# Weight halves moved from GpSimd to VectorE and ScalarE, and gathers one expert further ahead, in a routed FFN kernel

## The chip, the cores and the metric

The kernel runs on one core of a Trainium2 chip. The metric is the device time of one execution in microseconds (us). The core's engines each work through a queue of their own in program order: TensorE (PE in the profile; its weight loads are PEld), VectorE (DVE), ScalarE (ACT), GpSimd (POOL) and SyncE (SP, here only a queue of DMAs). They wait for each other through semaphores. The tensors are in HBM, the tiles in SBUF, and TensorE writes into PSUM.

## The reference

Three blocks follow each other: attention in chunks of 64 tokens, a layer of eight experts, and a plain FFN.

```python
x = attention_in_chunks(q, k, v)          # [2304, 512], all heads side by side
logits = x @ w_gate                       # 8 experts
e = argmax(logits); gate = softmax(logits)[e]
# token i is kept if fewer than capacity = 576 earlier tokens chose its expert
h = relu(x[tokens of e] @ w1[e])          # w1[e]: [512, 1024]
out[tokens of e] = gate * (h @ w2[e])     # w2[e]: [1024, 512]
h = out @ w_in                            # [2304, 2048]
y = (h * sigmoid(h)) @ w_out              # [2304, 512]
```

With the inputs of the reference the eight experts get 512, 128, 466, 384, 174, 128, 320 and 192 tokens: 4, 1, 4, 3, 2, 1, 3 and 2 tiles of 128, twenty in all.

## The kernel before

Everything is computed in fp16 pairs. A matrix is scaled by a power of two and split into a high half (rounded to fp16) and a low half (the rest), and each product is made of three matmuls: high by high, high by low, low by high. The power of two of a weight matrix comes from the sum of its squares. `w_prep(e, m, hi_eng, lo_eng)` returns the five steps of this for matrix m (0 is w1, 1 is w2) of expert e, each matrix in four chunks of [128, 1024]:

- `sq(c)`: ScalarE squares a chunk and sums along the row (L162);
- `red`: one TensorE matmul with ones adds the partitions (L122);
- `sc`: VectorE makes the scale from it (L168, L100 to L102), called the scale below;
- `hi(c)`: the high half of a chunk by `hi_eng` (L175 on ScalarE, L177 on another engine);
- `lo(c)`: the low half by VectorE (L180), from the chunk, the scale and the high half.

For expert 0 the high halves are made by ScalarE, for all others by GpSimd.

An expert's tokens are worked off in tiles of 128. `gather(e, j)` (L830) is an indirect DMA on GpSimd's queue that fetches the rows of tile j into a buffer `xg`. `x_tr(e, j)` transposes it by eight TensorE transposes (L842) into the one PSUM buffer `xtp`, which ScalarE copies to SBUF as `mxT` (L843). `t_f1` (L837) makes the rows' factor on VectorE. `tile_a(e, j)` is the upper tile, the first matrix: two halves of 48 matmuls (L858), each followed by ScalarE's Relu (`hh`, L863) and VectorE's rest (`hl`, L864). `tile_b(e, j)` is the lower tile, the second matrix: 24 matmuls of 512 columns (L884), then the eviction: a square for the norm (L893) and a scaled copy (L895) by ScalarE, the scale in between and the low half (L897) by VectorE, and a scatter on GpSimd's queue (L900).

The order is written out by hand (`manual_schedule`): what the text of the kernel issues first is first in each engine's queue. An expert runs as tile_a(0), tile_a(1), tile_b(0), tile_a(2), tile_b(1), and so on, under branches on its number of tokens (`more`); an expert with one tile runs tile_a(0), tile_b(0) and then the list `arms[0]`. Work for the next experts is put in between. `slots` are the places of the first tile: 0 ahead of tile_a, 1 after its first half, 2 after its end, 4 ahead of the last quarter of tile_b(e, 0), 5 behind it. `arms[j]` are the places of tile j: 0 to 2 within tile_a(j) likewise, 3 behind it, 5 behind tile_b(j−1). `nxt0(3)`, `nxt0(0)`, `nxt0(2)` and `nxt0(1)` come after tile_a's first half, after its end, at the middle and at the last quarter of tile_b(e, 0).

While expert e runs, the halves of expert e+1 are made (`hi1`, `lo1` of w1 and `hi2`, `lo2` of w2), and the squares of expert e+2 (`sq1`, `sq2`). `cb` and `cn` are pieces of the preparation of the FFN's first matrix: three VectorE operations (L805, L808, L813, a conversion) and ScalarE's norm (L819).

Of the kernel before, what the change touches and what calls it, by code (L numbers as in the profile page):

```python
# [8 lines left out]
F32 = mybir.dt.float32  # L9
# [13 lines left out]
def attention_moe_ffn_kernel(  # L23
# [617 lines left out]
    act_copy = nc.scalar.copy  # L641
    prep = {(1, m): w_prep(1, m, nc.gpsimd, nc.vector) for m in range(2)}
    p10 = prep[1, 0]
# [125 lines left out]
    mps = m_pool("mps", 1, space=PSUM)  # L769
    xg_s = [m_p.tile([P, XW], F32, name=f"xg{i}") for i in range(4)]  # L770
    xT_s = [m_p.tile([P, 2 * KD, P], F16, name=f"mxT{i}") for i in range(4)]
    f1_s = [m_p.tile([P, 1], F32, name=f"yf1{i}") for i in range(5)]
    hh_s = [m_p.tile([P, 4, P], F16, name=f"hh{i}") for i in range(4)]
# [23 lines left out]
    def f_conv(k):  # L797
        m, c = divmod(k, KFF)
        t = fs_s[k % 2]
        d = (win, wot)[m][:, c + 1, :]  # L800
        di = d.bitcast(I32)
        lo_w, hi_w = t[:, :, 0], t[:, :, 1]

        def b1():
            nc.vector.tensor_scalar(di, hi_w, 3, 0x3FFFFFFF, ALU.logical_shift_left, ALU.bitwise_and)  # L805

        def b2():
            nc.vector.scalar_tensor_tensor(  # L808
                out=di, in0=hi_w, scalar=-1073741824, in1=di, op0=ALU.bitwise_and, op1=ALU.bitwise_or
            )  # L810

        def b3():
            nc.vector.scalar_tensor_tensor(  # L813
                out=di, in0=lo_w, scalar=29, in1=di, op0=ALU.logical_shift_right, op1=ALU.bitwise_or
            )
            f_load(k + 2)

        def norm():
            nc.scalar.activation(  # L819
                out=(win, wot)[m][:, 0, :], in_=d, func=ACTF.Square, accum_out=fn2[:, m, c:c + 1]  # L820
            )

        return b1, b2, b3, norm
# [4 lines left out]
    def gather(e, j, idx):  # L828
        t = xg_s[2 * (e % 2) + j % 2]
        nc.gpsimd.indirect_dma_start(  # L830
            out=t, out_offset=None, in_=x_d[:, :], in_offset=bass.IndirectOffsetOnAxis(ap=idx, axis=0)
        )

    def t_f1(e, j):
        xg = xg_s[2 * (e % 2) + j % 2]
        f1 = f1_s[e % 2 if j == 0 else 2 + j % 3]
        nc.vector.tensor_scalar(f1, xg[:, DM:DM + 1], w_fac[e, 0], w_fac[e, 1], ALU.mult, ALU.mult)  # L837

    def x_tr(e, j):
        xh = xg_s[2 * (e % 2) + j % 2].bitcast(F16)  # L840
        for c in range(2 * KD):
# [29 lines left out]
    def tile_b(e, j, tok_i, c_i, keep, nxt, bg):  # L871
        f1, b = f1_s[e % 2 if j == 0 else 2 + j % 3], w_sp[e, 1]
        yp = yp_s[j % 2]
# [57 lines left out]

    g_next(0, 0)
    t_next(0, 0)
    g_next(0, 1)
    g_next(1, 0)
    w_load(1, 1)
    w_load(2, 0)
# [3 lines left out]
    for c in range(4):  # L941
        p10[3](c)
    n_e = [nc.values_load(cnt_i[0:1, e:e + 1], min_val=0, max_val=NT) for e in range(E)]

    for i in range(28):
        nc.tensor.matmul(out=ps_s[2][:, i % 4, :], lhsT=ones16, rhs=ident16)

    def more(e, j, arms, nxt0, bg0):
        def nxt(k):
            if k == 0 and j + 1 < NJ:  # L950
                x_tr(e, j + 1)
                t_f1(e, j + 1)
            if k == 0 and j + 2 < NJ:
                g_next(e, j + 2)
# [51 lines left out]
    for e in range(E):  # L1006
# [6 lines left out]
        if e + 2 < E:  # L1013
            for m in range(2):
                prep[e + 2, m] = w_prep(e + 2, m, nc.gpsimd, nc.vector)

# [13 lines left out]
        if not last:  # L1030
            sq1, sq2 = part(e + 2, 0, 0), part(e + 2, 1, 0)
            lo1, lo2 = los(0), los(1)
            hi1, hi2 = part(e + 1, 0, 3), part(e + 1, 1, 3)
            g2, gn = lambda: g_next(e, 2), lambda: g_next(e + 1, 1)
            if e == 0:
                sq = part(1, 1, 0)
                slots[1] = [lo1[0], *sq[0:2]]
                slots[2] = [*sq[2:4], gn, lambda: w_load(2, 1), *lo1[1:4]]
                slots[4] = [*scale(1, 1), *hi2]
                arms[0] = [*lo2, *sq1, *scale(2, 0), *sq2, *cb]  # L1040
                arms[1] = [[], [], [*cb[0:1]], [], [], [*lo2, *sq1]]
                arms[2] = [[], [], [*cb[1:]], [], [], [*scale(2, 0), *sq2]]
            else:
                slots[0] = [lambda: g_next(e + 1, 0), *hi1]
                slots[1] = [lo1[0], *sq1[0:2]]
                slots[2] = [*scale(e + 1, 1), g2, gn, *hi2, *sq1[2:4], *cn_prev, *lo1[1:4]]
                slots[5] = scale(e + 2, 0)
                arms[0] = [*lo2, *sq2, *cb]
                arms[1] = [lo2[0:1], [lo2[1], *sq2[0:2]], [*lo2[2:4], *sq2[2:4], *cb[0:1]], [], [], []]
                arms[2] = [[], [], [*cb[1:]], [], [], []]  # L1050
# [5 lines left out]
        def nxt0(k):  # L1056
            if k < 0:
                return
            if k == 3:
                x_tr(e, 1)  # L1060
            elif k == 2:
                if not last:
                    x_tr(e + 1, 0)
            elif k == 0:
                t_f1(e, 1)
                if last:
                    g_next(e, 2)
            elif not last:
                t_f1(e + 1, 0)
            else:  # L1070
                with tc.If(n_e[e] <= SPLIT0):
# [221 lines left out]
```

## Time and profile before

| | us |
|---|---|
| median of 3 runs | 858.53 (858.44 to 860.61) |
| profiled execution | 857.81 |
| its span, first to last instruction | 856.0 |
| mean granted clock of TensorE | 0.940 |
| busy: TensorE, VectorE, ScalarE, GpSimd | 731.6, 459.3, 358.9, 370.7 |

The attention and the routing end at about 146 us, the experts run to 443 us, and the FFN takes the rest. The granted clock is a share of 2.4 GHz: 1.00 is 2.4 GHz and 0.50 is 1.2 GHz. A row of the timeline gives the start, the duration, the engine, the line and the operation, the tiles (written from read), the shapes and the count; in brackets stands how long the engine was idle before it, and what ended that.

### The profile page before, as it was taken

To read this page: it belongs to the slowest core of one execution; us is meant where nothing else is said; L and a number is where in the kernel's file an instruction comes from. 1 tells how busy PE (TensorE), PEld (TensorE's weight loads), DVE (VectorE), ACT (ScalarE), POOL (GpSimd) and SP (SyncE) were. 2 spreads that over 40 slices of the span, in tenths; PEclk is the share of its full clock that TensorE was granted. 3 is DMA by queue.
4 is the path that set the end of the run, shared out by engine and by line. 5 is a ranking of instruction groups with operands and counts; after the bars stand their busy time and mean duration, and the time that the engine had idled before them with its cause. 6 is when DMAs were issued, how large, how long until landed. Compare 5 with 4: busy or idle time off the path is not lost. (4 is left out here: it accounts for less than half of the span.)

```text
span 856.0 us, 15037 instructions
## 1 busy us (share of the span) xinstructions
PE 731.6 (85%) x5750; PEld 444.2 (52%) x5750; DVE 459.3 (54%) x920; ACT 358.9 (42%) x643; POOL 370.7 (43%) x355
## 2 busy tenths in 40 slices
PE   5787753898789887869978777999999999999995
PEld 4676642875656655565733333444444444565442
DVE  4465586664992848699339999544332222212000
ACT  4586638475742726542424455332232223223010
POOL 3564541444961818486157644444223222312111
PEclk9899885899989998998999999899999999999998
DMA  7989891991892546433524246020001000000001
GB/s 168 235 227 202 193 234 39 342 348 46 275 292 63 185 166 198 145 99 87 129 59 98 67 131 148 1 49 1 1 26 50 0 1 38 13 1 38 13 34 41
DMA packets 103763, 95.94 MB, mean 112 GB/s; under 512 B 55904, under 2 KB 82528, under 8 KB 103648
## 3 DMA queue, kind: packets, MB, share of 16 engines
q1 hardware_dynamic: 97216, 76.07, 32.7%
q0 software_dynamic: 5760, 18.39, 6.6%
q8 instruction: 64, 1.05, 0.5%
q14 instruction: 51, 0.42, 0.2%
q10 hardware_dynamic: 672, 0.02, 0.0%
HBM read 73.45 MB, written 14.71 MB: 103 GB/s over the span
## 5 line engine op out<-in xcount | busy, mean ns | idle before, releaser
L1181 PE MATMUL ops<-wot,gh 128*128 128x512 f16 x576 | 171.3, 379 | 0.0
L1153 PE MATMUL fh<-yT,win 128*128 128x512 f16 (+1 forms) x768 | 157.7, 356 | 7.5 <-DVE g L1164 7.5
L1168 POOL TENSOR_TENSOR gl<-g,gh 128x512 f16<-128x512 f32 (+1 forms) x80 | 91.5, 1146 | 164.4 <-ACT gh L1166 164.4
L1153 PEld LDWEIGHTS <-win 128*128 128x128 f16 x960 | 94.5, 99 | 117.8 <-issue 26.2
L858 PE MATMUL mh<-mxT,wsp 128*128 128x128 f16 x1920 | 113.1, 220 | 8.8 <-ACT yr L893 4.1
L858 PEld LDWEIGHTS <-wsp 128*128 128x128 f16 x1920 | 110.5, 99 | 11.7 <-issue 10.4
L884 PE MATMUL myp<-wsp,hh 128*128 128x512 f16 x320 | 104.5, 411 | 12.6 <-issue 6.0
L1160 ACT ACTIVATE th<-th,fi 128x512 f32<-128x512 f32 (+1 forms) x80 | 54.3, 679 | 134.9 <-DVE th L1159 134.0
L1159 DVE TENSOR_TENSOR th<-fh,rb 128x512 f32<-128x512 f32 (+1 forms) x64 | 39.8, 622 | 131.1 <-PE fh L1153 131.1
L1181 PE MATMUL ops<-wot,gl 128*128 128x512 f16 x288 | 109.2, 379 | 0.0
L1181 PEld LDWEIGHTS <-gh 128*128 128x128 f16 x576 | 56.4, 98 | 64.1
L1166 ACT CAST gh<-g 128x512 f16<-128x512 f32 (+1 forms) x80 | 45.9, 574 | 76.5 <-DVE g L1164 57.6
L1164 DVE TENSOR_TENSOR g<-fh,th 128x512 f32<-128x512 f32 (+1 forms) x80 | 50.7, 634 | 39.9 <-ACT th L1160 32.1
L884 PE MATMUL myp<-wsp,hl 128*128 128x512 f16 x160 | 64.9, 406 | 0.0
L900 POOL DMA_INDIRECT y_d<-yr,tabs x20 | 21.4, 1070 | 94.3 <-DVE yr L892 30.9
L180 DVE SCALAR_TENSOR_TENSOR wsp<-st,s,wsp 128x1024 f16<-128x1024 f32 x40 | 60.4, 1551 | 2.1 <-POOL wsp L177 2.1
L177 POOL TENSOR_SCALAR wsp<-st,s 128x1024 f16<-128x1024 f32 x32 | 56.6, 1784 | 8.2 <-issue 7.5
L884 PEld LDWEIGHTS <-hh 128*128 128x128 f16 x320 | 32.4, 105 | 51.0 <-issue 17.4
L830 POOL DMA_INDIRECT xg<-x_d,tabs x34 | 44.3, 1304 | 26.9 <-issue 6.2
L1153 PE MATMUL fh<-st,win 128*128 128x512 f16 x192 | 43.4, 379 | 9.4 <-DVE g L1164 9.0
L180 DVE SCALAR_TENSOR_TENSOR wsp<-wot,s,wsp 128x1024 f16<-128x1024 f32 x24 | 44.9, 1916 | 8.2 <-POOL wsp L177 8.2
L1181 PEld LDWEIGHTS <-gl 128*128 128x128 f16 x288 | 28.2, 98 | 33.9
(201 smaller groups left out, 1013.3 us busy)
## 6 DMA issues: line engine op xcount, KB each, us to landing
st<-in_moe_w_dram SPq DMA_DIRECT2D x40, 512.0 KB, 4.6
wot<-in_moe_w_dram SPq DMA_DIRECT2D x24, 512.0 KB, 5.6
fs<-in_moe_w_in_dram SPq DMA_DIRECT2D x16, 512.0 KB, 7.4
fs<-in_moe_w_out_dram SPq DMA_DIRECT2D x16, 512.0 KB, 5.2
vbd<-in_v_dram SPq DMA_DIRECT2D x72, 64.0 KB, 3.9
x_d<-xr SPq DMA_DIRECT2D x9, 512.0 KB, 6.9
ku<-in_k_dram SPq DMA_DIRECT2D x6, 512.0 KB, 4.5
qu<-in_q_dram SPq DMA_DIRECT2D x6, 512.0 KB, 8.4
```

The lines of the kernel that those rows point to most:

```text
L177: hi_eng.tensor_scalar(sp[c][:, 0, :], st[c], s, 1.0, ALU.mult, ALU.mult)
L180: lo_eng.scalar_tensor_tensor(out=sp[c][:, 1, :], in0=st[c], scalar=s, in1=sp[c][:, 0, :], op0=ALU.mult, op1=ALU.subtract)
L830: nc.gpsimd.indirect_dma_start(out=t, out_offset=None, in_=x_d[:, :], in_offset=bass.IndirectOffsetOnAxis(ap=idx, axis=0))
L858: nc.tensor.matmul(out=ps[:, f4, :], lhsT=a[c][:, part, f0:f0 + P], rhs=xt[:, rc, :], start=(n == 0), stop=(n == 3 * KD - 1),)
L884: nc.tensor.matmul(out=yp, lhsT=lh[:, f % 4, :], rhs=b[f // 2][:, part, (f % 2) * DM:(f % 2 + 1) * DM], start=(n == 0), stop=(n == 3 * KF1 ...
L1153: nc.tensor.matmul(out=hp[:, 0:n], lhsT=wv[:, part, c, :], rhs=yT_t[b](rc, n), start=(i == 0), stop=(i == 3 * KD - 1),)
L1159: nc.vector.tensor_tensor(out=th[:, 0:n], in0=hp[:, 0:n], in1=rb_t[b][:, 0:n], op=ALU.mult)
L1160: nc.scalar.activation(out=th[:, 0:n], in_=th[:, 0:n], func=ACTF.Sigmoid, scale=fi[:, 0:1])
L1164: nc.vector.tensor_tensor(out=g[:, 0:n], in0=hp[:, 0:n], in1=th[:, 0:n], op=ALU.mult)
L1166: nc.scalar.copy(out=gh[:, 0:n], in_=g[:, 0:n])
L1168: nc.gpsimd.tensor_tensor(out=gl[:, 0:n], in0=g[:, 0:n], in1=gh[:, 0:n], op=ALU.subtract)
L1181: nc.tensor.matmul(out=o_t[b][t], lhsT=lh[:, t * P:(t + 1) * P], rhs=wv[:, part, :], start=(f == 0 and i == 0), stop=(f == KFF - 1 and i = ...
```

## The change

- High halves: of w1 by VectorE and of w2 by ScalarE, for experts 2 to 7; for expert 1, w1 by GpSimd as before and w2 by ScalarE.
- Gathers: six buffers `xg`, two for each of three experts. The first two tiles of expert e+2 and the third of e+1 are asked for at `nxt0(1)` of expert e, the fourth of e in its own slot 2.
- The transposes of expert e+1's second tile move into the last quarter of expert e's tile_b(e, 0), right behind those of the first tile at its middle. For that, `xT_s[0]` and `xT_s[2]` lie in parts of `win` and `wot`, and the norm of the conversion writes to `junk` instead.
- At the start both first gathers, the loads of the token counts into registers and the warm-up matmuls (48 instead of 28) come ahead of the first transposes.
- The order in the slots is written anew.

```diff
-    prep = {(1, m): w_prep(1, m, nc.gpsimd, nc.vector) for m in range(2)}
+    prep = {(1, m): w_prep(1, m, (nc.gpsimd, nc.scalar)[m], nc.vector) for m in range(2)}
...
-    xg_s = [m_p.tile([P, XW], F32, name=f"xg{i}") for i in range(4)]
+    xg_s = [m_p.tile([P, XW], F32, name=f"xg{i}") for i in range(6)]
+    xT_s = [None if i % 2 == 0 else m_p.tile([P, 2 * KD, P], F16, name=f"mxT{i}") for i in range(4)]
+    xT_s[0], xT_s[2] = (r.bitcast(F16).rearrange("p (c t) -> p c t", c=2 * KD) for r in (win[:, 0, :], wot[:, KFF, :]))
...
-                out=(win, wot)[m][:, 0, :], in_=d, func=ACTF.Square, accum_out=fn2[:, m, c:c + 1]
+                out=junk[:, 0:512] if m == 0 else wot[:, 0, :], in_=d, func=ACTF.Square, accum_out=fn2[:, m, c:c + 1]
...
     g_next(0, 0)
+    g_next(0, 1)
+    n_e = [nc.values_load(cnt_i[0:1, e:e + 1], min_val=0, max_val=NT) for e in range(E)]
+
+    for i in range(48):
+        nc.tensor.matmul(out=ps_s[2][:, i % 4, :], lhsT=ones16, rhs=ident16)
     t_next(0, 0)
-    g_next(0, 1)
     g_next(1, 0)
+    g_next(1, 1)
...
-            if k == 0 and j + 2 < NJ:
+            if k == 0 and j + 2 < NJ and (j > 1 or e + 1 == E):
                 g_next(e, j + 2)
...
-                prep[e + 2, m] = w_prep(e + 2, m, nc.gpsimd, nc.vector)
+                prep[e + 2, m] = w_prep(e + 2, m, (nc.vector, nc.scalar)[m], nc.vector)
...
             if e == 0:
                 sq = part(1, 1, 0)
-                slots[1] = [lo1[0], *sq[0:2]]
-                slots[2] = [*sq[2:4], gn, lambda: w_load(2, 1), *lo1[1:4]]
-                slots[4] = [*scale(1, 1), *hi2]
+                slots[1] = [lo1[0], sq[0]]
+                slots[2] = [g3, sq[1], lambda: w_load(2, 1), *lo1[1:4]]
+                slots[4] = [*sq[2:4], *scale(1, 1), *hi2]
                 arms[0] = [*lo2, *sq1, *scale(2, 0), *sq2, *cb]
-                arms[1] = [[], [], [*cb[0:1]], [], [], [*lo2, *sq1]]
-                arms[2] = [[], [], [*cb[1:]], [], [], [*scale(2, 0), *sq2]]
+                arms[1] = [[], [], [], [], [], [*lo2, *sq1, *cb[0:1]]]
+                arms[2] = [[], [], [*scale(2, 0)], [*sq2], [], [*cb[1:]]]
             else:
-                slots[0] = [lambda: g_next(e + 1, 0), *hi1]
-                slots[1] = [lo1[0], *sq1[0:2]]
-                slots[2] = [*scale(e + 1, 1), g2, gn, *hi2, *sq1[2:4], *cn_prev, *lo1[1:4]]
+                slots[0] = [hi1[0], hi1[1], lo1[0]]
+                slots[1] = [hi1[2], lo1[1], *sq1[0:1]]
+                slots[2] = [*scale(e + 1, 1), g3, hi1[3], *hi2[0:2], *lo1[2:4], *cn_prev]
+                slots[4] = [*sq1[1:4]]
                 slots[5] = scale(e + 2, 0)
-                arms[0] = [*lo2, *sq2, *cb]
-                arms[1] = [lo2[0:1], [lo2[1], *sq2[0:2]], [*lo2[2:4], *sq2[2:4], *cb[0:1]], [], [], []]
+                arms[0] = [*hi2[2:4], *lo2, *sq2, *cb]
+                arms[1] = [[], [], [], [*hi2[2:4], *lo2[0:2]], [], [*lo2[2:4], *sq2, *cb[0:1]]]
                 arms[2] = [[], [], [*cb[1:]], [], [], []]
...
             if k == 3:
-                x_tr(e, 1)
+                if e == 0:
+                    x_tr(e, 1)
...
             elif not last:
+                x_tr(e + 1, 1)
                 t_f1(e + 1, 0)
+                t_f1(e + 1, 1)
+                for g in ((e + 1, 2), (e + 2, 0), (e + 2, 1)):
+                    if g[0] < E:
+                        g_next(*g)
```

`g2`, `gn` and `g3` are gathers: the third tile of e, the second of e+1, and the fourth of e.

## Rows read from the trace of the kernel before

**Rows 1.** Groups of TensorE, 146 to 443 us: busy, mean ns, idle before, releasers.
```profile
L858 PE MATMUL mh<-mxT,wsp 128*128 128x128 f16 x1920 | 113.1, 220 | 8.8 <-ACT yr L893 4.1 <-DVE ye L100 3.1 <-ACT mxT L843 1.2
L884 PE MATMUL myp<-wsp,hh 128*128 128x512 f16 x320 | 104.5, 411 | 12.6 <-issue 6.0 <-ACT junk L162 3.4 <-POOL wsp L177 3.2
L842 PE MATMUL fh<-ident,xg 128*128 128x128 f16 x224 | 19.2, 235 | 23.0 <-DMA xg<-x_d,tabs 23.0
```

**Rows 2.** Timeline of TensorE at the start of the experts.
```profile
150.44 1.03 PE L842 MATMUL fh<-ident,xg 128*128 128x128 f16 x8 [4.47 <-DMA xg<-x_d,tabs]
...
153.88 3.08 PE L946 MATMUL mh<-ident,ones 128*128 128x128 f16 x28 [2.08 <-issue]
156.80 2.84 PE L858 MATMUL mh<-mxT,wsp 128*128 128x128 f16 x48
```

**Rows 3.** Timeline of TensorE, expert 2: transposes of the third tile.
```profile
238.32 1.04 PE L842 MATMUL fh<-ident,xg 128*128 128x128 f16 x8 [5.85 <-DMA xg<-x_d,tabs]
```

**Rows 4.** Stretches: us, busy of PE, PEld, DVE, ACT, POOL, PEclk, DMA share, GB/s.
```profile
239.10:243.20 4.10, 4.10 (x15) 1.59 (x13) 4.10 (x3) 3.21 (x5) 4.10 (x3) 0.63 0.91 311
243.60:246.25 2.65, 2.65 (x17) 1.33 (x15) 2.65 (x5) 1.01 (x1) 2.55 (x2) 1.00 0.90 267
...
sum 35.56, PE 35.52 PEld 16.70 DVE 34.92 ACT 19.11 POOL 33.58; mean PE 3.95 PEld 1.86 DVE 3.88 ACT 2.12 POOL 3.73
```

**Rows 5.** Timeline of VectorE, experts 0 and 1.
```profile
163.99 0.69 DVE L864 SCALAR_TENSOR_TENSOR hl<-mh,hh 128x512 f16<-128x512 f32 x1 [1.73 <-ACT hh L863]
...
164.77 3.67 DVE L180 SCALAR_TENSOR_TENSOR wsp<-st,s,wsp 128x1024 f16<-128x1024 f32 x3
...
169.74 0.42 DVE L805 TENSOR_SCALAR win<-fs 128x512 int32<-128x512 int32 x1
...
170.92 0.69 DVE L813 SCALAR_TENSOR_TENSOR win<-fs,win 128x512 int32<-128x512 int32 x1
...
208.29 4.31 DVE L180 SCALAR_TENSOR_TENSOR wsp<-wot,s,wsp 128x1024 f16<-128x1024 f32 x1 [1.61 <-POOL wsp L177]
```

**Rows 6.** Timeline of TensorE and GpSimd, expert 0, lower tile 0 to upper tile 3.
```profile
172.74 0.28 PE L122 MATMUL fh<-n,ones 128*128 128x4 f32 x2
...
173.76 6.54 POOL L177 TENSOR_SCALAR wsp<-st,s 128x1024 f16<-128x1024 f32 x4 [6.89 <-issue]
...
174.18 5.52 PE L858 MATMUL mh<-mxT,wsp 128*128 128x128 f16 x96
...
179.54 0.61 PE L842 MATMUL fh<-ident,xg 128*128 128x128 f16 x8
179.98 0.59 PE L884 MATMUL myp<-wsp,hh 128*128 128x512 f16 x2
...
185.16 0.28 PE L122 MATMUL fh<-n,ones 128*128 128x4 f32 x2
```

**Rows 7.** Two lines' instructions: duration in ns, least, median, most; first and last start.
```profile
L425 DVE TENSOR_SCALAR xr<-x,xs x4: 488/488/679, 119.6 to 130.8; 128x512 f16<-128x512 f32 x4
...
L175 ACT ACTIVATE wsp<-st,s x8: 1132/1137/1150, 91.1 to 149.3; 128x1024 f16<-128x1024 f32 x8
```

**Rows 8.** Timeline of ScalarE, expert 0, from the last copy in lower tile 0.
```profile
171.65 1.01 ACT L843 COPY mxT<-fh 128x1024 f16<-128x1024 f16 x1 [1.98 <-PE fh L842]
...
174.38 0.60 ACT L893 ACTIVATE yr<-myp 128x512 f16<-128x512 f32 x1 [1.72 <-PE myp L884]
...
176.12 1.05 ACT L162 ACTIVATE junk<-wot 128x1024 bf16<-128x1024 f32 x1
...
180.71 1.06 ACT L863 ACTIVATE hh<-mh 128x512 f16<-128x512 f32 x2
```

**Rows 9.** Line L122, the sum over squares: waits of its engine (us, times).
```profile
  ACT junk L162: 3.1, 3
```

**Rows 10.** Groups of VectorE, 146 to 443 us, columns as in rows 1.
```profile
L180 DVE SCALAR_TENSOR_TENSOR wsp<-st,s,wsp 128x1024 f16<-128x1024 f32 x36 | 54.9, 1570 | 2.1 <-POOL wsp L177 2.1
L180 DVE SCALAR_TENSOR_TENSOR wsp<-wot,s,wsp 128x1024 f16<-128x1024 f32 x24 | 44.9, 1916 | 8.2 <-POOL wsp L177 8.2
```

## What I expected before the run

> **What bounds the kernel now.** I began with the groups of TensorE in the expert stage (146 to 443 us), because the change touches nothing behind it. Between two experts, or within one, TensorE stands still in four ways. Transposes of gathered tokens wait for the gather, 23.0 us in all [rows 1]. 4.5 us of it is the very first gather [rows 2]; the other 18.5 us are five waits in experts 2, 3, 4 and 6, the longest 5.85 us [rows 1, 3]. Three waits are for the halves of weights: 3.2 in expert 1, 3.4 in expert 5 and 3.1 at the start of expert 6 [rows 1]. One is for a ScalarE copy, 1.2 [rows 1]. What is called issue comes back unchanged.
>
> Each of the seven longer waits leaves TensorE at the half level (1.2 of 2.4 GHz) for a while: twelve wide matmuls (or half an upper tile) take 4.10 us at a granted clock of 0.63, and 2.65 at 1.00 [rows 4]. Nine such stretches are 35.52 us together, two of them undisturbed (2.61 and 2.65); the seven slow ones are so 30.3 us where 18.6 would do, 11.7 lost [rows 4]: 7.2 behind gathers, 4.5 behind weights. Four transposes at the half level cost 0.4 each, 1.7.
>
> Next I looked at why weights and gathers are late. GpSimd makes the high halves, and VectorE's low half (two SBUF inputs) then takes 4.31 us, where three in a row alone take 3.67 [rows 5]. The gathers stand behind these halves in GpSimd's queue.
>
> **What the change takes away.** With gathers asked for an expert ahead, each has at least one lower and one upper tile (5.2 and 5.4 us [rows 6]) before its use, and GpSimd has nothing else from expert 1 on but scatters. I count all five waits as gone: 18.5 + 7.2 + 1.7 = 27.4. The three weight waits, with their clock: 3.2 + 3.4 + 3.1 + 4.5 = 14.2. The copy: 1.2. At the start the register loads (2.08) and the warm-up come ahead of the first transposes, so inside the 4.5 us wait. Before, 28 of them took 3.08 at the half level, and the level rose at 156.80 [rows 2]. Now they can start about 148.7; I let 48 end at 153.6 with the level risen, transposes at 154.1, a copy of 1.0, and the first tile at 155.2 for 156.80: 1.6 (0 if the level rises as late as before, 2.5 at best). Together 44.4 us.
>
> At this place a page speaks for the change: the Trainium skill, GPSIMD Engine Reference, Specifications, has GpSimd's SBUF interfaces shared with VectorE, in conflict with two-input instructions. The 4.31 us agree. The price is in the sum from the rows already.
>
> **What the change adds.** Four high halves of the first matrix per expert on VectorE. No such instruction of 1024 elements is in the trace; the same operation on 512 takes 0.488 [rows 7]. Bounds: 0.68 (twice it less a fixed part) and 1.2 (the pace of a low half); I take 0.7, nearest to the like operation. The Trainium skill, VectorE: DVE Perf Modes, section Mode 2×_2P, says that one-source fp32 between SBUF operands passes two results a cycle; 0.488 agrees. Four of the second matrix on ScalarE: exactly this instruction is there, 1.137, one begun every 1.04, so 4.3 for four [rows 7]. No total is too large; the order is what hurts. ScalarE works in order, and its queue holds the squares (1.15 each [rows 8]), the copies of transposes (1.0), the evictions and now the halves. TensorE waits for it in two places: the sum over the squares (L122, three waits already [rows 9]), and the next transposes, which need the one PSUM buffer `xtp` that the copy empties. The diff moves three squares to the last quarter of tile_b, behind them the second tile's copy, and the second matrix's halves behind VectorE's scale.
>
> Terms: half an upper tile 2.7, upper tile 5.36, transposes 0.45, lower tile 5.2, a quarter of it 1.3; matmul of sums to the next engine's start 1.02 [rows 6]. On VectorE: low half 1.2, hl 0.69, a conversion 0.42 + 0.73 + 0.69, with gaps 1.87 [rows 5]. Eviction on ScalarE 1.8 from its start to the next operation [rows 8].
>
> *Expert 0.* T is the last quarter of tile_b(0,0), 172.74 in the old trace; the copy before it ends then [rows 6, 8]. Squares 2 and 3 follow, so the sums wait to T+2.3: 2.3 lost. Scale, then four halves: T+3.4 to T+7.7; copy of expert 1's second tile to T+8.7; eviction to T+10.6; the four squares of expert 2 to T+15.4. TensorE goes on at T+2.7: transposes, the quarter, tile_a(0,2), transposes: T+10.1. There now stands the sum over those squares (formerly only after the next lower tile, at 185.16): 5.3 lost, and 1.3 for the clock. 8.9.
>
> *Experts 1 and 5 (one tile).* Count from the first matmul. VectorE ends the old eviction at 1.9, then two halves, a low half, hl, a half, a low half, hl: 7.8, scale 8.5. ScalarE's two halves wait for it and end at 10.7, two norms (0.7 each, squares of 512 columns like the eviction's 0.60 [rows 8]) 12.1, copy of the next expert's first tile 13.1. TensorE would transpose the second tile at 9.9: 3.2 lost. The three squares end at 16.7, TensorE's quarter, at half level, at 14.9: 1.8 lost. 5.0. In expert 5 VectorE is 3 us later (expert 4's last conversion and eviction): 2.5 before the lower tile, 3.85 and 1.75: 8.1.
>
> *Experts 2 and 6 (after one tile).* ScalarE comes with an eviction, two halves and four squares in hand: these end at 9.1, TensorE's upper tile at 5.4 (3.8 lost, 1.3 clock). VectorE has four low halves, two conversions, three high halves, two low, two hl before the scale: 3.0 + 4.8 + 3.7 + 2.1 + 2.4 + 1.4 + 0.7 = 18.1. ScalarE's halves, norms, two Relus and copy follow to 23.9; TensorE wants `xtp` at 19.4: 4.5. The next copy ends at 27.0, wanted at 25.7: 1.4. In expert 2 the squares end at 30.6, wanted at 28.9: 1.75. 12.8 and 11.0.
>
> *Experts 3 and 4.* Scale at 8.5 as in expert 1; TensorE has a second upper tile to do meanwhile, so 0.3 for `xtp`, then 1.45, then 1.75 for the squares: 3.5 each.
>
> *Expert 7* has no next expert: nothing. Transposes that move from one expert to the one before cost the same in both.
>
> **Sum.** New: 8.9 + 5.0 + 12.8 + 3.5 + 3.5 + 8.1 + 11.0 = 52.8. Removed: 44.4. Net +8.4 on the profiled execution's 857.8 gives 866.2; the median of the runs is 0.7 above that execution, so 867 us. The FFN behind it starts later by the same amount, with the same conversions left; its own waits stay. `xT` in `win` and `wot` is a change of place only; the norm's output in `junk` is written by the engine that writes it already.
>
> **Rivals.** (1) Faster: VectorE, freed from GpSimd, is so far ahead that the scale is there when ScalarE comes to the halves. VectorE's 60 low halves lose 28 us of contention (99.8 busy [rows 10] against 60 x 1.2) and take on 24 x 0.7 = 17. Then 3.2 in expert 1, 6.3 in expert 5, 6.0 in 2 and 6, and 1.7 in 3 and 4 vanish: 52.8 − 25 = 28, net −16, 842. For it: that surplus. Against it: the surplus lies in places where VectorE waits, in order, for ScalarE's evictions. The same goes for the page on GpSimd above: followed alone, it leads here. (2) Slower still: high halves at 1.2 on VectorE. It decides where the scale comes last: three halves ahead of it, 1.5 later, in six experts: +9, 876. Against it: 0.488. (3) About even: the half level does not follow the new waits (−3.9), and scale and squares come a little sooner than by my sums (−0.4 to −0.8 in each of six experts): 858 to 861. (4) The change does not do what it says: gathers that stand behind VectorE's factors (L837) are late again. They would have to be over 10 us late; I give it nothing apart.
>
> **Chances.** Forecast 0.60 (its own range 861 to 873), faster rival 0.18, slower still 0.12, about even 0.10. What a measurement here can tell from no change is 0.3%, 2.6 us. So faster 0.18, same 0.10, slower 0.72. For 8 in 10 the range takes the forecast, the even case and the slower one and part of the way to the faster: 853 to 877.
>
> **What would show it.** In the new trace: no wait of L842 for a gather after the first; low halves near 1.28 throughout; L177 on VectorE at about 0.75; the sum L122 after tile_a(0,2) waiting 5 us for ScalarE's squares; L842 waiting for the copy L843, in experts 2 and 6 by 4 to 5 us; ScalarE idle before L175 until VectorE's L102. Wrong if ScalarE does not wait before L175, or if L122 finds its squares done: then the removed 44 us stand alone and the kernel is much faster.

## The result and the profile after

The changed kernel takes 869.0 us (median, 866.5 to 870.3), 858.5 before: 1.0115 of it, with a 95% interval of 1.0082 to 1.0147. That is slower, as forecast, and 2 us from the 867.0. But that the number came out was luck, for it came of two wrong halves: what was taken away gave much less than the sum's 44 us, and what was added cost much less than its 53.

The profiled execution took 868.9 us (before: 857.8), its span 867.1. Line numbers have moved by one or two: what was L842, L843, L858, L884, L893 and L895 is now L843, L844, L859, L885, L894 and L896; the branches on an expert's number of tokens, L961 before, are L963. The first matmul of the experts comes at 156.27 us for 156.80, and the FFN begins at 454.4 for 443.4. The whole loss of 11 us so lies in the expert stage. The columns of the next rows are the stretch, its length, then busy time (and instructions) of TensorE, its weight loads, VectorE, ScalarE and GpSimd, the granted clock, DMA share and GB/s; the kernel before first.

```profile
156.80:443.42 286.62, 245.31 (x2656) 176.86 (x2653) 192.61 (x347) 141.63 (x261) 159.32 (x117) 0.93 0.54 175
```

The same of the changed kernel:

```profile
156.27:454.39 298.12, 246.00 (x2652) 176.53 (x2652) 177.09 (x371) 170.60 (x289) 68.46 (x67) 0.95 0.54 171
```

GpSimd lost 91 us of work, ScalarE got 29, VectorE lost 16 net. TensorE's busy time is the same within 0.7 us, so the loss is in its waits. Its groups in the changed kernel, 146 to 455 us (busy, mean ns, idle before, releasers), answer to [rows 1]; L859 has three rows now, since `xT` lies in three tiles.

```profile
L885 PE MATMUL myp<-wsp,hh 128*128 128x512 f16 x320 | 102.7, 405 | 16.9 <-issue 6.7 <-DVE wsp L180 3.3 <-DVE t L168 2.9
...
L859 PE MATMUL mh<-win,wsp 128*128 128x128 f16 x672 | 39.1, 219 | 2.1 <-ACT win L844 1.0 <-ACT yr L894 0.8 <-issue 0.3
L859 PE MATMUL mh<-mxT,wsp 128*128 128x128 f16 x672 | 38.5, 219 | 1.6 <-ACT yr L894 1.6
L859 PE MATMUL mh<-wot,wsp 128*128 128x128 f16 x576 | 36.4, 230 | 0.0
L843 PE MATMUL fh<-ident,xg 128*128 128x128 f16 x224 | 17.9, 225 | 10.2 <-ACT win L844 9.2 <-ACT mxT L844 1.0
L122 PE MATMUL fh<-n,ones 128*128 128x4 f32 x28 | 5.2, 254 | 20.2 <-ACT junk L162 20.2
L938 PE MATMUL mh<-ident,ones 128*128 128x128 f16 x48 | 4.4, 278 | 3.9 <-DVE tabs L709 3.9
```

The 23.0 us for gathers are gone. In their place the sums L122 wait 20.2 us for ScalarE's squares (0.1 before in this stretch; the 3.1 of [rows 9] lie outside it) and the transposes 10.2 us for ScalarE's copy (before, none did; the 1.2 there are upper tiles that waited for it). The waits ahead of the lower tile's matmuls, 6.6 of whose 12.6 us I had counted out, have not gone down but up, to 16.9.

The timeline of TensorE at the start, answering to [rows 2]: the warm-up stands ahead of the transposes, but it begins at 150.27 and not at 148.7. The row names VectorE's tables (L709) as the releaser. What ended last is something else: the eight loads of token counts into registers on TensorE's own queue (L935), which run from 146.90 to 150.25. The warm-up begins 4.1 us after the routing's last matmul (L691) here, and 1.9 in experiment 9, which has no such loads.

```profile
150.27 4.40 PE L938 MATMUL mh<-ident,ones 128*128 128x128 f16 x48 [3.91 <-DVE tabs L709]
154.51 0.61 PE L843 MATMUL fh<-ident,xg 128*128 128x128 f16 x8
```

The loads on TensorE's queue (ns least, median, most; first and last start):

```profile
L935 PEldq TENSOR_LOAD <-cnt_i x8: 300/306/499, 146.9 to 149.9; - x8
```

In expert 0, answering to [rows 6], the two sums wait where the prediction put them, 2.03 and 4.03 us:

```profile
174.41 0.39 PE L122 MATMUL fh<-n,ones 128*128 128x4 f32 x2 [2.03 <-ACT junk L162]
...
186.94 0.39 PE L122 MATMUL fh<-n,ones 128*128 128x4 f32 x2 [4.03 <-ACT junk L162]
```

In expert 2, the same view: a wait for squares, an upper tile that runs 7.15 us for 5.52, and a wait for the copy out of `xtp`. The transposes of the third tile, which waited 5.85 us for a gather in [rows 3], come at 244.68 without a wait; those that wait for the copy, at 251.94, are of expert 3's first tile.

```profile
237.45 0.38 PE L122 MATMUL fh<-n,ones 128*128 128x4 f32 x2 [3.54 <-ACT junk L162]
237.70 7.15 PE L859 MATMUL mh<-wot,wsp 128*128 128x128 f16 x96
244.68 0.61 PE L843 MATMUL fh<-ident,xg 128*128 128x128 f16 x8
...
251.94 0.61 PE L843 MATMUL fh<-ident,xg 128*128 128x128 f16 x8 [4.06 <-ACT win L844]
```

The cause of the second wait stands in ScalarE's timeline of that stretch. ScalarE sits idle for 7.06 us until VectorE has the second matrix's scale (L101), then makes two halves (L175), two norms and two Relus, and only then the copy that TensorE has wanted since 247.9.

```profile
246.46 2.19 ACT L175 ACTIVATE wsp<-st,s 128x1024 f16<-128x1024 f32 x2 [7.06 <-DVE s L101]
248.56 0.61 ACT L820 ACTIVATE junk<-win 128x512 bf16<-128x512 f32 x1
...
249.92 1.06 ACT L864 ACTIVATE hh<-mh 128x512 f16<-128x512 f32 x2
250.88 1.01 ACT L844 COPY win<-fh 128x1024 f16<-128x1024 f16 x1
```

### The profile page after: what moved, and what is told of

The parts are those of the page before. It is cut to its first block, busy times and chain, and to the rows that moved or that the text cites. A ratio compares the mean times of both kernels' runs of the same rounds, so it can differ in the third digit from the quotient of the medians.

```text
span 867.1 us, 14949 instructions
## 1 busy us (share of the span) xinstructions
PE 735.1 (85%) x5770; PEld 446.6 (52%) x5770; DVE 443.8 (51%) x944; ACT 388.2 (45%) x671; POOL 280.8 (32%) x305
## 5 line engine op out<-in xcount | busy, mean ns | idle before, releaser
L885 PE MATMUL myp<-wsp,hh 128*128 128x512 f16 x320 | 102.7, 405 | 16.9 <-issue 6.7
L859 PEld LDWEIGHTS <-wsp 128*128 128x128 f16 x1920 | 112.2, 100 | 6.7 <-issue 4.8
L831 POOL DMA_INDIRECT xg<-x_d,tabs x36 | 38.2, 1060 | 112.4 <-issue 80.1
L885 PE MATMUL myp<-wsp,hl 128*128 128x512 f16 x160 | 64.5, 403 | 0.7 <-issue 0.7
L885 PEld LDWEIGHTS <-hh 128*128 128x128 f16 x320 | 31.8, 103 | 52.9 <-issue 21.8
L180 DVE SCALAR_TENSOR_TENSOR wsp<-st,s,wsp 128x1024 f16<-128x1024 f32 x40 | 50.6, 1300 | 0.0
L162 ACT ACTIVATE junk<-st 128x1024 bf16<-128x1024 f32 x40 | 42.2, 1056 | 3.7 <-DMA st<-in_moe_w_dram 3.0
L100 DVE TENSOR_SCALAR ye<-yn 128x1 int32<-128x1 int32 x20 | 3.1, 154 | 79.2 <-ACT yr L894 79.2
L859 PE MATMUL mh<-win,wsp 128*128 128x128 f16 x672 | 39.1, 219 | 2.1 <-ACT win L844 1.0
```

Source lines behind the costliest of these rows:

```text
L162: nc.scalar.activation(out=junk, in_=st[c], func=ACTF.Square, accum_out=n2[:, c:c + 1])
L180: lo_eng.scalar_tensor_tensor(out=sp[c][:, 1, :], in0=st[c], scalar=s, in1=sp[c][:, 0, :], op0=ALU.mult, op1=ALU.subtract)
L831: nc.gpsimd.indirect_dma_start(out=t, out_offset=None, in_=x_d[:, :], in_offset=bass.IndirectOffsetOnAxis(ap=idx, axis=0))
L859: nc.tensor.matmul(out=ps[:, f4, :], lhsT=a[c][:, part, f0:f0 + P], rhs=xt[:, rc, :], start=(n == 0), stop=(n == 3 * KD - 1),)
L885: nc.tensor.matmul(out=yp, lhsT=lh[:, f % 4, :], rhs=b[f // 2][:, part, (f % 2) * DM:(f % 2 + 1) * DM], start=(n == 0), stop=(n == 3 * KF1 ...
```

## The experiments

Each was run beside the kernel before on the same chip; ratios are to that kernel, with 95% intervals. Where two experiments on different chips are compared, these ratios are compared. The changed kernel is at 1.0115.

**1. The gathers alone.** The kernel before with six gather buffers, gathers an expert ahead and `xT` as in the change; halves on GpSimd, lists in the old order.

```diff
-    xg_s = [... for i in range(4)]
+    xg_s = [... for i in range(6)]
-                slots[0] = [lambda: g_next(e + 1, 0), *hi1]
+                slots[0] = [*hi1]
+                for g in ((e + 1, 2), (e + 2, 0), (e + 2, 1)): g_next(*g)      # in nxt0(1)
```

> The kernel before with the change's gathers alone: six buffers, tokens asked for an expert ahead; the halves stay on GpSimd, slots and transposes stay where they were. Theory (TensorE's five gather waits, 18.5 us, and the half clock behind them were worth their price, and the new order gave it back): those waits go, but VectorE's hl comes next in experts 2 and 6, so not all 27 us come back: 838 us, between 832 and 846. Rival (the gathers hid nothing, because the halves are as late as the gathers): 855 to 860.

Measured: 846.1 us, 0.985 (0.981 to 0.989). Waits for gathers fall from 23.0 to 6.2, 4.5 of it the first. The gathers are worth 13 us by themselves, so the rest of the change costs some 23. They are worth less than expected, since TensorE then waits elsewhere. The waits of TensorE, 146 to 450 us (us, times, longest); the 3.3 put down to GpSimd's half and the 2.5 stand at branches of experts 5 and 1, on which experiments 8 and 9 have more:

```profile
PE fh L843 <- DMA xg<-x_d,tabs: 6.2, 3, 4.5
PE myp L885 <- issue: 4.8, 3, 3.0
...
PE myp L885 <- POOL wsp L177: 3.3, 1, 3.3
PE myp L885 <- DVE win L814: 3.3, 2, 3.0
PE myp L885 <- DVE wsp L180: 2.5, 1, 2.5
```

**2. ScalarE without the wait for the scale.** The changed kernel, with the second matrix's halves split by the first matrix's scale of the same expert, which is there earlier. The squares, the sum and the second scale are still made, but not used for the split.

> The changed kernel, with the second matrix's halves of experts 1 to 7 split by the scale of the same expert's first matrix, which is ready long before; the squares, their sum and the second scale are still made. It takes away only what ScalarE's high halves wait for. Theory (ScalarE stands still before its high halves until VectorE's scale comes, 28.7 us in all, and holds the copies that free the transposes' buffer): the waits of the transposes for the copy (10.2) go, and part of those of the sums and of the half clock: 853 us, between 848 and 859. Rival (ScalarE has simply too much to do): 865 to 869.

Measured: 855.1 us, 0.995 (0.991 to 0.998), 1.7% or 14 us under the changed kernel. All waits of transposes for the copy vanish, those for the squares stay:

```profile
PE fh L122 <- ACT junk L163: 18.3, 9, 3.5
```

So the wait for the scale costs by the path that the prediction names, the copy out of `xtp`, and the squares are a cost of their own.

**3. Expert 0's squares in another order.** The changed kernel with the squares that its second sum needs moved ahead.

```diff
-                slots[1] = [lo1[0], sq[0]]
-                slots[2] = [g3, sq[1], lambda: w_load(2, 1), *lo1[1:4]]
-                slots[4] = [*sq[2:4], *scale(1, 1), *hi2]
+                slots[1] = [lo1[0], *sq[0:2]]
+                slots[2] = [g3, *sq[2:4], lambda: w_load(2, 1), *lo1[1:4]]
+                slots[4] = [*scale(1, 1), *hi2]
-                arms[2] = [[], [], [*scale(2, 0)], [*sq2], [], [*cb[1:]]]
+                arms[2] = [[], [], [], [], [], [*scale(2, 0), *sq2, *cb[1:]]]
```

> The changed kernel with expert 0's lists as before the change in two respects: the squares of expert 1's second matrix in slots 1 and 2, and the sum over expert 2's squares behind the next lower tile. Theory (two sums in expert 0 wait 2.0 and 4.0 us for squares and leave the half level for 1.7): 861 us, between 859 and 863, and nothing of it is taken back later. Rival (ScalarE is behind anyway, and the wait turns up at the next sum or copy): 866 to 870.

Measured: 862.8 us, 1.005 (1.003 to 1.008); waits for squares 14.2 in seven, so both of expert 0's (6.1 us) are gone, by order alone. By the ratios 5 us of its 7.7 come back; a branch at the end of expert 0, which cost nothing in the changed kernel, is exposed by 1.7 us here.

**4. The second matrix's halves back on GpSimd.** The changed kernel with `(nc.vector, nc.gpsimd)[m]` (and GpSimd for both matrices of expert 1), its lists unchanged.

> The changed kernel with the second matrix's high halves back on GpSimd, the first matrix's on VectorE as changed. Theory (the second matrix's halves in ScalarE's queue make the loss): ScalarE's copies and squares come earlier, the waits for them shrink by 10 to 20 us, VectorE's low halves beside GpSimd's halves take some of it: 856 us, between 850 and 862. Rival (the high halves on VectorE make the loss): 865 to 870.

Measured: 862.4 us, 1.004 (1.001 to 1.007), less gain than expected. Waits for squares fall to 10.9, but waits for low halves and `hl` of VectorE come up, 3.6 and 3.4 us. GpSimd in the change's order is little better than ScalarE.

**5. Squares of the next-but-one expert earlier.**

```diff
-                slots[1] = [hi1[2], lo1[1], *sq1[0:1]]
-                slots[2] = [*scale(e + 1, 1), g3, hi1[3], ...]
-                slots[4] = [*sq1[1:4]]
+                slots[1] = [hi1[2], lo1[1], *sq1[0:2]]
+                slots[2] = [*sq1[2:4], *scale(e + 1, 1), g3, hi1[3], ...]
```

> The changed kernel with the squares of expert e+2's first matrix back in slots 1 and 2, ahead of the scale, for experts 1 to 6; nothing else. ScalarE then makes them while it would stand still before its high halves. Theory (TensorE's sums wait for squares that stand too late in ScalarE's order; five waits of 1.0 to 1.5 us, and the 3.7 us at the branch behind one of them with the half level after it): 857 us, between 853 and 862. Rival (ScalarE is full, and the squares only push Relus and copies back): 865 to 870.

Measured: 865.5 us, 1.0025 (0.9993 to 1.0056), 0.9% or 8 us under the changed kernel. The time lies in the rival's range, but the kernel before took 861.8 on this chip; 1.0025 of its 858.5 elsewhere is 861, at the theory's upper end. Four waits for squares remain (11.1 us), and the waits for the copy stay (9.6).

**6. Gathers, and the first matrix's halves on VectorE.** Experiment 1 with `(nc.vector, nc.gpsimd)[m]` for experts 2 to 7.

> The gathers alone (846 us) with, in addition, the first matrix's high halves of experts 2 to 7 on VectorE; the second matrix's stay on GpSimd, the order stays that of the kernel before. Theory (what is left in experts 1, 5 and 6 there are low halves of the first matrix that stand beside GpSimd's high halves, three waits of 2.5 to 3.3 us with the half level behind them): 834 us, between 829 and 841. Rival (VectorE, with four more instructions of 0.74 us for each expert, becomes late itself): 844 to 850.

Measured: 844.3 us, 0.980 (0.976 to 0.984). The waits of 2.8 and 3.3 us ahead of the lower tile in the one-tile experts 1 and 5 are still there, with GpSimd relieved of half its work. So the theory is out: relief of the halves alone does not remove them. The time is at the rival's, but its cause, a late VectorE, is not shown either; experiments 8 and 9 have another. Against experiment 1 the intervals overlap. Beside experiment 4, which has the same engines, it prices the change's order, with its moved transposes and its start, where GpSimd makes the second matrix's halves: 0.980 against 1.004. The moved transposes were not run alone.

**7. Both orders mended, second halves behind the second upper tile.** Experiments 3 and 5 together, and all of `hi2` in `arms`, a tile later.

> The changed kernel with its engines and gathers, but three things put in another order: expert 0's lists as in the run with expert 0's order, the squares early as in the run with squares early, and all four high halves of the second matrix behind the second upper tile (or, with one tile, behind the lower tile), where the scale is there. Theory (the loss is the order alone; the sums' waits of 20 us and most of the 10 us of the transposes go, with some of the half level): 843 us, between 837 and 851. Rival (the engines are at fault: ScalarE and VectorE do not keep up with the halves in any order): 856 to 868.

Measured: 855.0 us, 0.993 (0.991 to 0.996), between theory and rival: order alone gives back 1.8%, some 16 us, and not all that the theory wants. Waits for squares are down to 10.3 us, two of 5 us in experts 2 and 6, and those for the copy to 7.5.

**8 and 9. No branches.** In both kernels the numbers of tokens are written in, and the tests made when the program is built, for all engines. The tests of the last expert on the first tiles of the FFN and the code for experts with more than five tiles are left out with them. The edit, the same for both:

```diff
-        with tc.If(n_e[e] > P * j) as cmp:
+        if COUNTS[e] > P * j:          # [512, 128, 466, 384, 174, 128, 320, 192]
             tile_a(e, j, nxt, bg)
...
-        with cmp.Else():
+        else:
             tile_b(e, j - 1, *cols(e, j - 1), *before)
```

> The kernel before, with the numbers of tokens per expert written into it, so that no engine branches on them in the expert loop (what is left out: the reading of the counts for the tests, the tests themselves, and the code of experts with more than five tiles). Theory (the waits of TensorE ahead of the second matrix where the test sends it to the Else arm, 3.17, 0.86, 3.41 and 3.56 us in experts 1, 4, 5 and 7 and 10.7 us over all of the taken branches, are the branch itself, during which the queue fetches nothing): those waits go, and 858 becomes 846 (840 to 850), the rest of the gain being matmuls at the half level behind them. Rival (they are waits for the halves of the second matrix on GpSimd, as the prediction had it): waits of 2.5 us or more stay at experts 1 and 5, and the time is 855 to 859.

> The changed kernel with the numbers of tokens per expert written into it in the same way (the same parts left out). Theory (branches): the 16.7 us that TensorE stands at its eight taken branches in the changed kernel go, and the matmuls at the half level behind those of experts 3, 4 and 7 get back up to 5 us: 850 (843 to 854). The waits for the squares at the sums stay at 12 to 20 us, those for the copy of the transposes at 7 to 10. Rival (halves on VectorE and ScalarE are late): 864 to 870, with waits of 2.5 us or more ahead of the second matrix.

The reason for them stands in the rows of the branch itself (TensorE's sequencer: ns least, median, most). Before, the line and the one of expert 1:

```profile
L961 PEldq COMPARE_BRANCH  x26: 65/184/5074, 161.6 to 438.0; - x26
...
L961 PEldq COMPARE_BRANCH  x1: 3908/3908/3908, 207.6 to 207.6; - x1
```

In the changed kernel the line, and the one of expert 4:

```profile
L963 PEldq COMPARE_BRANCH  x26: 65/245/6515, 161.1 to 452.2; - x26
...
L963 PEldq COMPARE_BRANCH  x1: 4006/4006/4006, 348.4 to 348.4; - x1
```

A test that goes on to the next tile takes under 0.1 us; the one in each expert that jumps to the Else arm takes 3.6 to 5.1 us before and 3.3 to 6.5 in the change. What of this TensorE feels depends on the matmuls still queued ahead of it. Before, the jump at 207.6 has 1.0 us of them, and 3.17 us are lost; that of expert 0 (at 192.4, 3.75 us) has 4.0 us, the last 17 of a lower tile's 24 wide matmuls, and nothing is lost. In no run of this case do more than 17 matmuls start during a long jump, however many the program has ahead of it: 17 of 512 columns last 4.0 us, 17 of 128 columns 1.2. Over the eight jumps TensorE stands 11 us before and 17 in the change. Of the 5.7 us more, 2.8 are expert 4's, which has next to nothing queued, and 3.7 those of experts 3 and 6, whose jumps take 6.5 and 5.1 us behind a lower tile (4.05 and 3.75 before); the others give 0.9 back.

Measured: 846.5 us, 0.983 (0.978 to 0.987) for the kernel before, and 850.6 us, 0.988 (0.983 to 0.992) for the changed one, both at the theory's number (846 and 850). In the traces, the expert stage from the first matmul to the FFN takes 278.2 for 286.6 and 281.9 for 298.1: 8 and 16 us. The trace of the kernel before without branches is of its longest run, 851.8 us, and its waits for gathers are 5.7 us longer than with them. Some of the rest came from the start, where no counts are read into registers: from the routing's last matmul, the experts' first comes 1.8 and 1.5 us sooner. So without branches the change costs 4 us, within what the two intervals leave open, and with them 10.5.

But the trace is no plain win for the theory. The timeline of TensorE in expert 1, kernel before without branches:

```profile
207.19 0.34 PE L122 MATMUL fh<-n,ones 128*128 128x4 f32 x2
207.39 0.59 PE L884 MATMUL myp<-wsp,hh 128*128 128x512 f16 x2
...
212.94 0.39 PE L884 MATMUL myp<-wsp,hl 128*128 128x512 f16 x1 [1.93 <-DVE hl L864]
...
216.88 0.34 PE L858 MATMUL mh<-mxT,wsp 128*128 128x128 f16 x3 [1.02 <-DVE wsp L180]
218.94 1.33 PE L858 MATMUL mh<-mxT,wsp 128*128 128x128 f16 x11 [1.72 <-DVE wsp L180]
```

The lower tile follows at once where it waited 3.17 us [rows 1], so that wait was the branch. Then 4.7 us of waits for VectorE's work come in its place: two causes stood one behind the other. Expert 1 gets 3.2 us shorter and expert 2 longer, and the two together gain nothing by losing one cause (75.0 us for 73.3). Expert 5 is alike (2.7 us at `hl`, and as much for a gather). The gain is in experts 4 and 7, where nothing is late behind the branch: they take 3.3 and 5.3 us less. The changed kernel without branches, same place:

```profile
210.84 0.34 PE L122 MATMUL fh<-n,ones 128*128 128x4 f32 x2
211.04 0.59 PE L885 MATMUL myp<-wsp,hh 128*128 128x512 f16 x2
...
218.98 1.01 PE L843 MATMUL fh<-ident,xg 128*128 128x128 f16 x8 [3.41 <-ACT win L844]
```

In expert 1 VectorE is not late here at all, and what comes in the branch's place is the copy out of `xtp`, 3.41 us: the prediction has 3.2 there. In all, waits for the copy rise from 10.2 to 19.4 us, and those for squares fall to 12.5; for the copy 7 to 10 were foreseen. In the change with its branches, a wait can also stand right ahead of a jump. In expert 4, TensorE waits 1.51 us for squares with nothing queued behind, and the jump that follows is exposed by 3.68 us:

```profile
348.38 0.38 PE L122 MATMUL fh<-n,ones 128*128 128x4 f32 x2 [1.51 <-ACT junk L162]
352.44 1.04 PE L885 MATMUL myp<-wsp,hh 128*128 128x512 f16 x2 [3.68 <-issue]
```

The Trainium skill, Runtime: NRT & Kernel Launch, section Instruction fetch mechanics, says that a taken branch whose target lies outside what has been fetched makes the engine wait for a fetch. The trace agrees. During each of the eight jumps, of either kernel, one packet of 16 KB moves on q8, a queue of instructions: it starts 1.0 to 4.1 us into the jump, and the jump ends 1.3 to 1.5 us after the packet has landed (once 2.35). No test that falls through has such a packet. In the changed kernel, the queues' packets, MB and share of the 16 DMA engines during expert 3's jump of 6.5 us (313.90 to 320.42), where the packet starts 4.1 us in:

```profile
q1 hardware_dynamic: 1213, 1.67, 78.0%
q0 software_dynamic: 80, 0.26, 16.9%
q8 instruction: 1, 0.02, 0.9%
```

During expert 2's of 3.3 us (276.69 to 280.03), where it starts 1.0 us in, it is the only packet of any queue:

```profile
q8 instruction: 1, 0.02, 1.7%
```

That other transfers hold the packet back is likely by these two, but no run varies them alone.

**10. The fifth gather earlier.** Experiment 6 still had two waits for the gather of a fifth tile.

```diff
-            if k == 0 and j + 2 < NJ and (j > 1 or e + 1 == E):
-                g_next(e, j + 2)
+            if k == 0 and j == 1:
+                if e + 1 == E:
+                    g_next(e, 3)
+                g_next(e, 4)
```

> The best one so far (the kernel before with the gathers one expert ahead, and the first matrix's halves of experts 2 to 7 on VectorE; 844.3 us), with the gather of an expert's fifth tile started in its second tile, right behind the transposes of the third. Theory: the two waits of 1.5 and 1.0 us ahead of the fifth tile's transposes in experts 0 and 2 go, and nothing else changes: 842 (838 to 844.5). Rival: GpSimd reaches the gather earlier and makes the second matrix's halves behind it later, or the rows land beside weights that then land later: 844 to 848.

Measured: 836.6 us, 0.971 (0.967 to 0.976), better than expected and the fastest kernel with its branches: 3% under the kernel before. Both waits are gone. Why it gained some 0.9% and not 0.3% isn't settled; its interval and experiment 6's nearly touch.

**11. The test ahead of the first tile.** Experiment 10, with the first tile's code in both arms, so that 24 wide matmuls of the expert before stand ahead of the jump.

```diff
-        tile_a(e, 0, nxt0, bg0)
-        more(e, 1, arms, nxt0, bg0)
+        first = lambda: tile_a(e, 0, nxt0, bg0)
+        more(e, 1, arms, nxt0, bg0, first)     # first() begins both arms; experts 1 to 7
```

> The best one so far (gathers one expert ahead, the first matrix's halves on VectorE, the fifth tile's gather early; 0.971 of before), with the test for an expert's second tile put ahead of its first tile, whose code then stands in both arms, for experts 1 to 7. Theory (a taken branch costs TensorE 3.5 to 5 us less what its queue still holds; ahead of this test now stand 24 matmuls of 512 columns of the expert before, 5.3 us of work, and not matmuls of 128 columns, some 1 us): the waits of 2.7 and 3.6 us ahead of the second matrix in the one-tile experts 1 and 5 go and come back nowhere, those in experts 3, 4 and 7, whose taken test stays, do not: 0.964 of before (0.960 to 0.968). Rival (the jump at the end of the expert before and this branch now stand one behind the other, and the sum is longer than the queue): the waits stand ahead of the first tile's first matmul, with 0.970 to 0.975.

Measured: 845.2 us, 0.985 (0.982 to 0.989): slower than experiment 10 by 1.4%, the rival, and worse than it said. The waits inside experts 1 and 5 do go, but one of 3.54 and one of 8.85 us stand ahead of these experts. In the trace, two jumps follow each other there, 6.65 and 5.88 us at expert 5, more than the queued matmuls cover:

```profile
L968 PEldq COMPARE_BRANCH  x2: 5879/6264/6650, 331.2 to 338.0; - x2
```

and TensorE's timeline over the same stretch:

```profile
334.74 0.38 PE L888 MATMUL myp<-wsp,hl 128*128 128x512 f16 x1
343.97 1.33 PE L862 MATMUL mh<-mxT,wsp 128*128 128x128 f16 x11 [8.85 <-issue]
```

**12. The second matrix's halves on ScalarE, in the old order.** Experiment 10 with `(nc.vector, nc.scalar)[m]`.

> The best one so far with the high halves of the second matrix of experts 2 to 7 on ScalarE in the place of GpSimd, in the order of the lists of before: one part of the change alone. Theory (what the change loses is ScalarE's queue, whatever the order: four halves of 1.14 us stand ahead of a ReLU or a copy, and wait for the scale): waits for the copy of the transposes and for ReLU of 1 to 4 us come up in the experts with several tiles, 0.98 of before (0.976 to 0.99). Rival (the loss is only in the order that the change gives the lists, and GpSimd's halves were in VectorE's way): the time stays at 0.971 or falls, 0.963 to 0.972.

Measured: 878.7 us, 1.022 (1.018 to 1.027), 42 us over experiment 10 and further than the theory's end. The waits of TensorE, and of ScalarE for the scale, 146 to 450 us:

```profile
PE fh L843 <- ACT win L844: 26.1, 3, 12.3
PE fh L843 <- ACT mxT L844: 6.2, 1, 6.2
...
ACT wsp L175 <- DVE s L101: 17.2, 6, 8.9
...
ACT wsp L175 <- DVE inv L102: 6.7, 1, 6.7
```

Four halves in a row (4.26 us), behind a scale that isn't there, and after them squares, norms and Relus stand ahead of the copy. With the change's order, which splits them in twos and moves the scale, and its other parts it is 869.0 for 878.7. So the order is not bad in itself: it suits ScalarE's halves and costs where GpSimd makes them (experiments 4 and 6). What the engine of the second matrix's halves costs depends on the order: 0.971 to 1.022 in the old one (experiments 10 and 12), the largest single step here, and 1.004 to 1.0115 in the change's (experiment 4).

## Why the prediction was right, point by point

- *Gathers, 18.5 us removed: right.* No transposes wait for one any more, and in experiment 1, which has the gathers alone, all but 1.7 us of it go.
- *Clock, 11.7 and 1.7 us removed and 3.9 added: wrong.* TensorE's busy time is 245.3 before and 246.0 after. The half level went where the gathers had been and came back behind the new waits and exposed jumps: two lower tiles take 7.02 and 8.26 us for 5.34, two upper ones 7.15 each for 5.52, and nine matmuls of a lower tile in expert 3 3.56 for 2. Behind the waits where the 3.9 were put, in experts 0, 2 and 6, it is 1.7 + 1.6 + 1.6 = 4.9; what the sum lacks is the half level behind the exposed jumps. The stretches of the changed kernel, columns as above, answer to [rows 4]:

```profile
187.19:194.21 7.02, 7.02 (x29) 2.88 (x29) 4.28 (x12) 6.07 (x11) 0.35 (x1) 0.76 1.04 349
237.70:244.85 7.15, 7.15 (x102) 7.15 (x102) 7.05 (x11) 1.71 (x4) 0.00 (x0) 0.76 1.06 374
320.56:324.12 3.56, 3.56 (x9) 1.26 (x10) 0.10 (x2) 0.00 (x0) 1.02 (x1) 0.54 0.48 164
352.44:360.70 8.26, 8.26 (x24) 3.08 (x25) 3.99 (x6) 3.05 (x6) 0.61 (x1) 0.64 0.76 225
```

- *Three weight waits, 9.7 us: the step that failed.* I took late halves for the one cause of all three, though [rows 1] names a half only at the first, 3.2, and a square at the second, 3.4. At these two a branch stood too. In expert 1 the change makes VectorE's work early, as forecast, and the branch keeps TensorE waiting 2.88 there and 3.31 in expert 5 all the same. Only the third, 3.1 at the start of expert 6, went. What is called issue, which I put down as unchanged, was mostly branches too: 4.6 of its 6.0 us, in experts 3, 4 and 7. Over all jumps TensorE loses 5.7 us more than before, which stood nowhere in the sum.
- *Copy, 1.2, and start, 1.6:* the copy's wait became 10.2. The start gave 0.53 (0.9 from the end of the routing, which came 0.4 later). I took the 2.08 us of idle time in [rows 2] for the length of the register loads; the eight take 3.35, and the warm-up stands behind them.
- *VectorE's price: right.* High halves take 0.74 us (0.7 taken), low halves 1.28 at the median (1.2) and 1.76 at most, against up to 4.31 [rows 5, 7, 10]. The rows of the two lines (ns least, median, most):

```profile
L177 DVE TENSOR_SCALAR wsp<-wot,s x12: 739/744/752, 213.2 to 371.2; 128x1024 f16<-128x1024 f32 x12
...
L180 DVE SCALAR_TENSOR_TENSOR wsp<-st,s,wsp x40: 1267/1278/1758, 99.5 to 411.9; 128x1024 f16<-128x1024 f32 x40
L180 DVE SCALAR_TENSOR_TENSOR wsp<-wot,s,wsp x24: 1272/1278/1299, 214.5 to 386.6; 128x1024 f16<-128x1024 f32 x24
```

- *Expert 0, 8.9: right*, 2.03 + 4.03 + 1.7 for the slow tile, 7.7.
- *Experts 2 and 6, 12.8 and 11.0: right in kind and nearly in size.* 3.54 + 1.6 + 4.06 + 1.03 = 10.2, and 3.54 + 1.6 + 4.04 = 9.2. VectorE's scale was put 18.1 us after expert 2's first matmul; it is there at 246.4, 18.0 after it.
- *Experts 1 and 5, 5.0 and 8.1: right in kind for a kernel without branches, too high by 10 for this one.* Only the waits for squares came, 1.51 each. The branch holds TensorE for 2.9 and 3.3 us, and ScalarE's copy is done meanwhile. Experiment 9 has the missing ones: 3.41 for 3.2 in expert 1, and 3.38, 3.31 and 0.57 for 2.5, 3.85 and 1.75 in expert 5; the 1.8 for squares in expert 1 do not come there. *Experts 3 and 4, 3.5 each:* 2.9 and 2.2.
- *The sum.* Without clock, removed was put at 31.0; it is 18.5 + 3.1 + 0.5 = 22.1, and branches take 5.7 back. Clock was put at −9.5 net; it is +0.7. New waits were put at 48.9; they are 20.1 for squares and 9.0 more for the copy, 29.1. So −16.4 + 0.7 + 29.1 = 13.4, less some 2 of small waits gone, for +8.4 forecast and 11.1 measured. Errors of some 25 and 20 us cancelled: luck, in part because the branches that kept the old waits hid the new ones.
- *The faster rival* needed ScalarE to find its scale ready. It sat idle 28.7 us ahead of L175 in all, 25.9 of them put down to L101. Experiment 2 shows what it would have given: 14 us, not 25.

## What to carry to other kernels

A wait can have two causes one behind the other, and the profile names one: look at the sequencer's rows for compare-and-branch and register loads, and at what is queued on the array ahead of them, before you count a wait as removed. In a queue that works in order, work moved to a less busy engine costs by what stands behind its operand's wait, not by its duration: 24 halves of 1.13 us on ScalarE cost 42 us in experiment 12. The gathers, the fifth tile's early, and the first matrix's halves alone gave a kernel 3% faster than before, where the whole change was 1.2% slower.

## What the runs showed of the hardware that I had not expected

In these two kernels a jump to an Else arm took TensorE 3.3 to 6.5 us, some 40 times and more a test that falls through (0.06 to 0.09), while on VectorE, ScalarE and GpSimd no test of this line took more than 0.08 us. Two in a row add up: 12.5 us at expert 5 in experiment 11. The long part is a packet of 16 KB on an instruction queue, with the jump's end 1.3 to 1.5 us behind its landing in all but one of these sixteen. The jump is free only behind enough queued matmuls, and no more than 17 started after a jump had begun, in any run: behind a lower tile (17 of 512 columns, 4.0 us) jumps of 3.3 to 3.9 us cost nothing, and those of 5.1 and 6.5 us 1.26 and 2.63; behind an upper tile (17 of 128 columns, 1.2 us at most) every one was exposed, as the 3.17 us of [rows 1] show.
